# The first remainder's products ahead of two blocks of packs, and a remainder's output rows split by partitions between two engines

## The chip, the cores and the metric

The kernel runs on one core of one Trainium2 chip. The metric is the device time of one execution in microseconds (us), the median of several runs. A core has five engines that run side by side and wait for each other on semaphores: TensorE (PE in the profile, with its weight loads as PEld), VectorE (DVE), ScalarE (ACT), GpSimd (POOL) and SyncE (SP), which here only issues transfers. Transfers are carried out by 16 DMA engines that the issuing queues share.

## The reference

```python
def sm_attn(qq, kk, vv):
    s = scale * np.matmul(qq, kk.transpose(0, 1, 3, 2))
    s = s - np.max(s, axis=-1, keepdims=True)
    a = np.exp(s)
    a = a / (np.sum(a, axis=-1, keepdims=True) + 1e-09)
    return np.matmul(a, vv)
p_packed = sm_attn(p, k, v)
out = sm_attn(q, p_packed, p_packed)
...
x = out.transpose(0, 2, 1, 3).reshape(B * S, H * D)
h = x @ w_in
g = h * (1.0 / (1.0 + np.exp(-h)))
return g @ w_out
```

There are 8 batches of 8 heads, 576 tokens a batch, 64 elements a head, 32 packs a head; the model width is 512 and the inner width 2048. All arrays are fp32. Each head's 32 pack queries attend to all tokens, then all tokens attend to the 32 packed results; a two-layer network with a SiLU between follows on every token.

## The kernel before, in words

**Packs and h.** The second attention's values are multiplied with `w_in` before they are weighted: `Packs.products` (through `heads`, L232) makes "packs", the packed values of a batch times a quarter (512 columns, 4 blocks of 128) of `w_in`. A block of packs fills one `ps_two` tile, of which there are two (two PSUM banks each). `Packs.upper` (L490, ACT) rounds it to an upper part `pw_hi`, `Packs.lower` (L493, DVE) writes the difference `pw_lo`; both read the tile, which is free after that. `h_products` (L525) multiplies packs with the token shares `a_hi`, `a_lo` and gives one 128-row block of h for all tokens of a batch. Products of fp32 precision are made of three products of rounded parts: upper with upper, upper with lower, lower with upper.

**Units.** A unit is a pair (batch, block f of 128 inner columns). A batch's 576 tokens are taken as two halves of 288; of each half the first 256 tokens (MAIN) go through `h_values` (L543, L545, ACT: g and its upper part g_hi) and `h_lower` (L551, DVE: g_lo), and the 32 left over (REST) are put aside in `rest`. `out_products` (L561) multiplies g with `w_out`, summing over the 16 blocks in two `ps_acc` tiles. For each pair of batches the tokens left over, 2 x 2 x 32 = 128, make up a remainder: four units of four blocks each, whose g lies ready in `rest`. For them `h_values` only copies g to g_hi (L535, ACT), `h_lower` makes g_lo (L551, DVE), and `out_products` issues 4 x 3 products into one bank. There are four remainders, those of batches 0, 2, 4 and 6 with the batch after each.

**Order.** The order of PE, DVE, ACT and SP is that of the program text. The first 32 units (all of batches 0 and 1) follow the list ORDER, written by hand; its end is `o30 o31 g32 b1 l32 v3 e31.0 pp11 pu11 e31.1 pl11 k3`: the output products of the last units, g_hi and g_lo of unit 32 (the first unit of the first remainder), the output rows, the packs of batch 2, quarter 0, and a load. After that a loop takes the units from 32 on (`n_early`). Unit 32 stands first there: `packs_in(2, 1, 2)` makes quarters 1 and 2 of batch 2 (both products, then upper and lower of each), then come its output products. For unit 33 `hidden_up_to(35)` first issues g_hi and g_lo of units 33, 34 and 35, then its output products follow. With unit 34 the h products of batch 2 begin (unit 36).

**Output rows of a remainder.** After its fourth unit `out_rows` copies the 128 rows of 512 columns from the bank to a tile `o`: the left 256 columns by ACT (L595), the right 256 by DVE (L596). Rows 0 to 31 are batch b, first half; 32 to 63 batch b, second half; then the same for batch b + 1. Four transfers (L600) of 32 rows each, 64 KB, write them to `out`; all on SP, except in the last remainder, where two of them are issued by ACT. The last remainder is the last work of the kernel.

Of the kernel before, what the change touches and what calls it, by code (L numbers as in the profile page):

```python
# [20 lines left out]
B, H, S, D = 8, 8, 576, 64  # L21
NP = 32
NI = H // 2
HS = S // 2
NB = HS // 32
DM = H * D
# [7 lines left out]
MAIN = HS // P * P  # L34
REST = HS - MAIN
# [48 lines left out]
def packed_attention_ffn(ctx: ExitStack, tc: tile.TileContext, pkT, qT, v, w_in, w_out, out):  # L84
# [13 lines left out]
    nc = tc.nc  # L98
# [32 lines left out]
    def sum_banks():  # L131
        return ps_acc.tile([P, 2, 512], F32, name="ps_acc")
# [333 lines left out]
    class Packs:  # L466
# [5 lines left out]
        def products(self):  # L472
            self.ps = two_banks()
            heads(
                lambda par: self.ps[:, par, : self.nf * P].rearrange("p (f n) -> p f n", n=P),
                made["packs", self.b],
                lambda r, i: win[r, self.f : self.f + self.nf, i].bitcast(F32),
            )
# [19 lines left out]
    n_early = len(units)  # L498
# [9 lines left out]
    def half_or_all(hf):  # L508
        return slice(0, 2) if hf is None else slice(hf, hf + 1)

    def h_products(u, hf=None):
        b, f, *more = units[u]
        ps = made["h", u, hf] = two_banks()
        p_hi, p_lo = made["pw", b, f // FJ]
        cols = slice(f % FJ * P, f % FJ * P + P)
        for h in range(2)[half_or_all(hf)]:
            if u < WHOLE:
                terms = ((p_hi.bitcast(F32), made["whole", h]),)
            else:
                a_hi, a_lo = made["a2", b, h]  # L520
                terms = (p_hi, a_hi), (p_hi, a_lo), (p_lo, a_hi)
            todo = [(p, a, par) for par in range(2) for p, a in terms]
            for n, (p, a, par) in enumerate(todo):
                bank = ps[:, h if hf is None else 0, :HS]
                nc.tensor.matmul(bank, p[:, par, cols], a[:, par], start=(n == 0), stop=(n == len(todo) - 1))  # L525

    def h_values(u, hf=None):
        b, f, *more = units[u]
        if hf is None or hf == 0:
            pool = gp_b if u > n_early and (u - n_early) % 3 == 1 else gp  # L530
            g_hi = pool.tile([P, 512], F32R, name="g_hi")
            g_lo = pool.tile([P, 512], F32R, name="g_lo")
            if more:
                g = rest[:, f : f + FJ].rearrange("p f e h s -> p (f e h s)")
                nc.scalar.copy(g_hi, g)  # L535
                hidden[u] = g, g_hi, g_lo
                return
            hidden[u] = g_hi.bitcast(F32) if u < WHOLE else gp.tile([P, 512], F32, name="g", bufs=1), g_hi, g_lo
        g, g_hi = (x.rearrange("p (h s) -> p h s", h=2) for x in hidden[u][:2])
        ps, to = made.pop(("h", u, hf)), rest[:, f, b % 2]  # L540
        if hf is not None:
            ps, to, g, g_hi = ps[:, 0], to[:, hf], g[:, hf], g_hi[:, hf]
        nc.scalar.activation(g, ps[..., :MAIN], AF.Silu)  # L543
        if u >= WHOLE:
            nc.scalar.activation(g_hi, ps[..., :MAIN], AF.Silu)  # L545
        nc.scalar.activation(to, ps[..., MAIN:HS], AF.Silu)  # L546

    def h_lower(u, hf=None):
        c = slice(0, 512) if hf is None else slice(256 * hf, 256 * hf + 256)
        g, g_hi, g_lo = hidden[u][-3:]  # L550
        nc.vector.tensor_tensor(g_lo[:, c], g[:, c], g_hi[:, c].bitcast(F32), ALU.subtract)  # L551
# [11 lines left out]
    def is_last(u):  # L563
        return u + 1 == len(units) or units[u + 1][0] != units[u][0] or len(units[u + 1]) > len(units[u])

    def first_of(u):

        while u and not is_last(u - 1):
            u -= 1
        return u  # L570

    def out_products(u, hf=None):
        b, f, *more = units[u]
        start = first_of(u)
        first = u == start
        if more:
            if first:
                acc[start, 0] = sum_banks()
            for n in range(FJ):
                products(acc[start, 0][:, 0], u, f + n, n, f + n == 0, f + n == NF - 1)  # L580
            return
        for h in range(2)[half_or_all(hf)]:
            if first:
                acc[start, h] = sum_banks()
            for k in range(2):
                products(acc[start, h][:, k], u, f, 2 * h + k, first, is_last(u))

    def out_rows(u, h):

        b, f, *more = units[u]  # L590
        sums = acc[first_of(u), h]
        if more:
            o = osb.tile([P, 2, DM], F32, name="o")
            half = DM // 2
            nc.scalar.copy(o[:, 0, :half], sums[:, 0, :half])  # L595
            nc.vector.tensor_copy(o[:, 0, half:], sums[:, 0, half:])  # L596
            for n, (e, h) in enumerate((e, h) for e in range(2) for h in range(2)):
                at = (b + e) * S + h * HS + MAIN
                rows = slice((2 * e + h) * REST, (2 * e + h) * REST + REST)
                (nc.scalar if n % 2 and b == B - 2 else nc.sync).dma_start(out[at : at + REST], o[rows, 0])  # L600
            return
        if ("o", b, h) in outs:
            o = outs.pop(("o", b, h))
            nc.vector.tensor_tensor(o, sums, o, ALU.add)
        else:
            o = osb.tile([P, 2, DM], F32, name="o")
            (nc.vector.tensor_copy if h else nc.scalar.copy)(o, sums)
        if f == NF - 1:
            at = b * S + h * HS
            nc.sync.dma_start(out[at : at + MAIN].rearrange("(k p) e -> p k e", p=P), o)  # L610
        else:
            nc.sync.dma_start(parts[b, h], o)

    def load_parts(b):
# [24 lines left out]
        "l": h_lower,  # L639
        "o": out_products,  # L640
        "e": out_rows,
        "b": load_parts,
    }
# [18 lines left out]
    def hidden_up_to(u):  # L662
        nonlocal done
        while done < min(u, len(units) - 1):
            done += 1
            if len(units[done]) == 2:
                h_products(done)
            h_values(done)
            h_lower(done)

    def packs_in(b, *quarters):
        both = [Packs(b, FJ * j, FJ) for j in quarters]
        for part in both:
            part.products()
        for part in both:
            part.upper()
            part.lower()
# [39 lines left out]
    for u in range(n_early, len(units)):  # L717
        b, f, *more = units[u]
        if more:
            if u == n_early:  # L720
                packs_in(2, 1, 2)
            else:
                hidden_up_to(u + 2)
            out_products(u)
            if f + FJ == NF:
                out_rows(u, 0)
            continue
        step = STEPS_AT.get(f) if b + 1 < B else None
        all_banks = step in ("scores1", "scores2") or f == PACKS_OWN or f == PACKS_NEXT and b + 1 < B
        if not all_banks:  # L730
            hidden_up_to(u + 2)
        if f == PACKS_OWN:
            packs_in(b, *((3,) if b == 2 else (2, 3)))
        if f == PACKS_NEXT and b + 1 < B:
            packs_in(b + 1, 0, 1)
        if step:
            step_of(b + 1, step)
        out_products(u)
        if f == NF - 1:
            for h in range(2):  # L740
                out_rows(u, h)
        if step == "packed":
            attention[b + 1].turned()
            attention[b + 1].packs()
# [43 lines left out]
```

## Time and profile before

| | |
|---|---|
| median of 3 runs | 710.75 us (709.83 to 710.82) |
| the profiled execution, its own time | 710.59 us |
| its span | 708.8 us |
| mean granted clock of TensorE | 0.996 |
| PE busy | 696.7 us, 98% |
| DVE busy / ACT busy | 332.4 us (47%) / 328.5 us (46%) |
| transfers in all | 65.20 MB |

The span reaches from the first to the last instruction of the profiled execution; its own time is 1.8 us longer. In the lines of a view L561 is line 561 of the kernel; "x12" counts instructions merged into a line; a bracket gives how long the engine stood idle before it and who released it. SPq and ACTq are the queues that issue transfers. Times within the span are counted from its start.

### The profile page before, as it was taken

Reading aid. Unit: us, or ns where it says so; the run is one execution under the profiler, and the core shown is the slowest. Engines: PE = TensorE matmul, PEld = TensorE weight load, DVE = VectorE, ACT = ScalarE, POOL = GpSimd, SP = SyncE. Lnnn points to the kernel's source line nnn. Section 1 sums busy time; section 2 is a strip of 40 time slices with the busy share of each in tenths; the row PEclk is TensorE's granted clock in tenths of the full one; section 3 lists DMA queues with packets and bytes.
Section 4 is the critical chain, followed back from the end, with each engine's and each line's share of the span. In section 5 each row is a group of like instructions: output and inputs, shape, how many; then the busy total and the mean of one; then the engine's idle time right before and its main releaser. Section 6 shows DMA issues by size and latency. Waiting matters only on the chain.

```text
span 708.8 us, 12103 instructions
## 1 busy us (share of the span) xinstructions
PE 696.7 (98%) x5060; PEld 564.7 (80%) x5060; DVE 332.4 (47%) x491; ACT 328.5 (46%) x614; POOL 21.0 (3%) x16
## 2 busy tenths in 40 slices
PE   8999999999999999999999999999999999999997
PEld 6647779877868888888888888878878788888886
DVE  4989985944642346332552315433362333622112
ACT  4896858634534325362542625453353533533221
POOL 0202020100000000000000000000000000000000
PEclk9999999999999999999999999999999999999999
DMA  9755653315032140302212022121301210010002
GB/s 356 304 205 198 222 218 149 125 60 193 0 130 82 34 147 1 127 21 84 75 60 83 18 88 75 41 87 36 144 1 64 79 35 2 1 59 1 1 1 74
DMA packets 30869, 65.20 MB, mean 92 GB/s; under 512 B 19296, under 2 KB 19296, under 8 KB 26464
## 3 DMA queue, kind: packets, MB, share of 16 engines
q1 hardware_dynamic: 30720, 64.30, 25.1%
q8 instruction: 40, 0.66, 0.4%
q10 hardware_dynamic: 96, 0.13, 0.1%
q14 instruction: 13, 0.11, 0.0%
HBM read 48.76 MB, written 11.53 MB: 85 GB/s over the span
## 4 chain that ended last, share of the span: by engine, by line
PE 91%; DVE 5%; ACT 2%; issue 1%; DMA 1%; DVEq 0%; ACTq 0%
PE ps_acc L561 55%; PE ps_two L525 27%; PE ps_two L232 6%; PE ps_two L330 1%; DVE win L198 1%; DMA kvq_t<-in_pkT 1%; PE ps_acc L232 0%; ACT tm L278 0%; DVE win L204 0%; ACT w_raw L192 0%; ACT w_raw L193 0%; DVE w_raw L198 0%; ACT L543 0%; DVE win L197 0%; DVE win L205 0%
## 5 line engine op out<-in xcount | busy, mean ns | idle before, releaser
L561 PE MATMUL ps_acc<-wo_hi,g_hi 128*128 128x512 f32 x560 | 222.5, 397 | 0.0
L561 PE MATMUL ps_acc<-wo_lo,g_hi 128*128 128x512 f32 x560 | 219.0, 391 | 0.0
L561 PE MATMUL ps_acc<-wo_hi,g_lo 128*128 128x512 f32 x560 | 219.0, 391 | 0.1
L551 DVE TENSOR_TENSOR g_lo<-g,g_hi 128x512 fp32r<-128x512 f32 x124 | 89.2, 720 | 256.5 <-ACT g_hi L545 256.4
L543 ACT ACTIVATE g<-ps_two 128x512 f32<-128x512 f32 x124 | 74.4, 600 | 265.4 <-PE ps_two L525 236.4
L525 PE MATMUL ps_two<-a_lo,pw_hi 128*128 128x288 f32 x528 | 156.2, 305 | 0.2
L525 PE MATMUL ps_two<-a_hi,pw_hi 128*128 128x288 f32 x496 | 147.1, 297 | 1.0 <-ACT rest L546 1.0
L525 PE MATMUL ps_two<-a_hi,pw_lo 128*128 128x288 f32 x496 | 145.9, 294 | 0.0
L561 PEld LDWEIGHTS ps_acc<-wo_hi,g_hi 128*128 128x128 f32 x560 | 105.1, 188 | 38.7 <-issue 19.4
L561 PEld LDWEIGHTS ps_acc<-wo_hi,g_lo 128*128 128x128 f32 x560 | 105.1, 188 | 23.7 <-DVE g_lo L551 0.8
L561 PEld LDWEIGHTS ps_acc<-wo_lo,g_hi 128*128 128x128 f32 x560 | 105.2, 188 | 18.0
L525 PEld LDWEIGHTS ps_two<-a_lo,pw_hi 128*128 128x128 f32 x528 | 99.2, 188 | 6.8 <-ACT rest L546 0.9
L525 PEld LDWEIGHTS ps_two<-a_hi,pw_hi 128*128 128x128 f32 x496 | 93.3, 188 | 5.6 <-ACT rest L546 1.3
L525 PEld LDWEIGHTS ps_two<-a_hi,pw_lo 128*128 128x128 f32 x496 | 93.2, 188 | 0.0
L545 ACT ACTIVATE g_hi<-ps_two 128x512 fp32r<-128x512 f32 x124 | 73.6, 593 | 7.8 <-PE ps_acc L561 7.8
L493 DVE TENSOR_TENSOR pw_lo<-ps_two,pw_hi 128x1024 fp32r<-128x1024 f32 x31 | 36.8, 1219 | 9.5 <-ACT pw_hi L490 9.5
L490 ACT CAST pw_hi<-ps_two 128x1024 fp32r<-128x1024 f32 x31 | 30.2, 1019 | 16.0 <-PE ps_two L232 16.0
L232 PE MATMUL ps_two<-win,ppT 64*32 64x512 f32 (+1 forms) x560 | 32.7, 559 | 2.6 <-DVE pw_lo L493 1.6
L546 ACT ACTIVATE rest<-ps_two 128x64 f32<-128x64 f32 (+1 forms) x132 | 30.4, 230 | 0.0
L232 PEld LDWEIGHTS ps_two<-win,ppT 64*32 64x32 f32 x560 | 8.2, 105 | 17.8 <-issue 10.3
L543 ACT ACT_TABLE_LOAD x16 | 20.5, 1283 | 2.0 <-PE ps_two L525 1.9
L535 ACT CAST g_hi<-rest 128x512 fp32r<-128x512 f32 x16 | 9.9, 623 | 14.1 <-PE ps_acc L561 13.7
(116 smaller groups left out, 479.4 us busy)
## 6 DMA issues: line engine op xcount, KB each, us to landing
kvq_t<-in_v SPq DMA_DIRECT2D x8, 1280.0 KB, 6.4
kvq_t<-in_pkT SPq DMA_DIRECT2D x7, 1216.0 KB, 6.9
out<-o SPq DMA_DIRECT2D x16, 512.0 KB, 2.8
kvq_t<-in_qT SPq DMA_DIRECT2D x7, 1152.0 KB, 5.2
w_raw<-in_w_in SPq DMA_DIRECT2D x6, 1024.0 KB, 6.4
win<-in_w_out SPq DMA_DIRECT2D x3, 1024.0 KB, 5.7
w_raw<-in_w_out SPq DMA_DIRECT2D x3, 1024.0 KB, 4.8
tm<-tm SPq DMA_DIRECT2D x56, 40.0 KB, 1.9
```

Of the source, the lines that this page charges most:

```text
L198: nc.vector.scalar_tensor_tensor(low, up, -(2**31), low, op0=ALU.bitwise_and, op1=ALU.bitwise_or)
L232: nc.tensor.matmul(bank(par)[NP * i : NP * i + NP], lhs(r, i), rhs(r, i), start=True, stop=True)
L330: nc.tensor.matmul(self.ps[NP * i : NP * i + NP, par * D : par * D + D], e, vs[:n, c, h * D : h * D + D], start=(c == 0), stop=(c == 4),)
L490: nc.scalar.copy(self.hi, self.ps[:, :, : self.nf * P])
L493: nc.vector.tensor_tensor(self.lo, self.ps[:, :, : self.nf * P], self.hi.bitcast(F32), ALU.subtract)
L525: nc.tensor.matmul(bank, p[:, par, cols], a[:, par], start=(n == 0), stop=(n == len(todo) - 1))
L535: nc.scalar.copy(g_hi, g)
L543: nc.scalar.activation(g, ps[..., :MAIN], AF.Silu)
L545: nc.scalar.activation(g_hi, ps[..., :MAIN], AF.Silu)
L546: nc.scalar.activation(to, ps[..., MAIN:HS], AF.Silu)
L551: nc.vector.tensor_tensor(g_lo[:, c], g[:, c], g_hi[:, c].bitcast(F32), ALU.subtract)
L561: nc.tensor.matmul(bank, g[:, rows], w[:, at], start=(first and n == 0), stop=(last and n + 1 == len(todo)))
```

## The change

It has two parts. In the loop over units, unit 32's output products are issued before `packs_in(2, 1, 2)` and not after it. In `out_rows` a remainder's rows are split by partitions and not by columns: rows 0 to 63 (batch b) are copied whole by ACT, rows 64 to 127 (batch b + 1) by DVE, and each 64 rows leave with one transfer, whose destination is written as halves x 32 tokens x 512 columns. In the last remainder ACT issues the first of the two, elsewhere SP issues both.

```diff
@@ -591,13 +591,11 @@
         sums = acc[first_of(u), h]
         if more:
             o = osb.tile([P, 2, DM], F32, name="o")
-            half = DM // 2
-            nc.scalar.copy(o[:, 0, :half], sums[:, 0, :half])
-            nc.vector.tensor_copy(o[:, 0, half:], sums[:, 0, half:])
-            for n, (e, h) in enumerate((e, h) for e in range(2) for h in range(2)):
-                at = (b + e) * S + h * HS + MAIN
-                rows = slice((2 * e + h) * REST, (2 * e + h) * REST + REST)
-                (nc.scalar if n % 2 and b == B - 2 else nc.sync).dma_start(out[at : at + REST], o[rows, 0])
+            for e in range(2):
+                rows = slice(2 * e * REST, 2 * e * REST + 2 * REST)
+                (nc.vector.tensor_copy if e else nc.scalar.copy)(o[rows, 0], sums[rows, 0])
+                to = out[(b + e) * S : (b + e) * S + S].rearrange("(h s) e -> h s e", s=HS)[:, MAIN:]
+                (nc.sync if e or b < B - 2 else nc.scalar).dma_start(to, o[rows, 0])
             return
         if ("o", b, h) in outs:
             o = outs.pop(("o", b, h))
@@ -717,11 +715,11 @@
     for u in range(n_early, len(units)):
         b, f, *more = units[u]
         if more:
+            if u > n_early:
+                hidden_up_to(u + 2)
+            out_products(u)
             if u == n_early:
                 packs_in(2, 1, 2)
-            else:
-                hidden_up_to(u + 2)
-            out_products(u)
             if f + FJ == NF:
                 out_rows(u, 0)
             continue
```

## The prediction

> **What bounds the kernel now.** First the page's busy times, then the chain of waits, then the timeline where the two parts of the change lie: the change of stage near 194 us and the end.
>
> ```profile
> span 708.8 us, 12103 instructions
> PE 696.7 (98%) x5060; PEld 564.7 (80%) x5060; DVE 332.4 (47%) x491; ACT 328.5 (46%) x614; POOL 21.0 (3%) x16
> ```
>
> PE is busy nearly always. The chain of waits over 204.6 to 704.4 us, grouped by line, says how strictly:
>
> ```profile
> by line: PE ps_acc L561 61.4%; PE ps_two L525 30.6%; PE ps_two L232 6.2%; PE ps_two L330 1.7%; PE ps_two L349 0.1%
> ```
>
> For 500 us the chain is PE alone. A delay of PE before 204.6 us therefore comes out at the end in full, and so does a gain. What may move the time is a stall of PE ahead of that, or the work behind the last product. The chain at the change of stage:
>
> ```profile
> 195.41 1.02 ACT pw_hi L490
> 196.43 0.03 issue
> 196.46 1.23 DVE pw_lo L493
> ...
> 198.83 5.71 PE ps_acc L561 x24
> ```
>
> Here the chain leaves PE for ACT and DVE. The same stretch in the timeline, three engines together:
>
> ```profile
> 192.08 0.69 DVE L551 TENSOR_TENSOR g_lo<-rest,g_hi 128x512 fp32r<-128x512 f32 x1 [0.69 <-ACT g_hi L535]
> 194.21 1.95 PE L232 MATMUL ps_two<-win,ppT 64*32 64x512 f32 x32
> 195.41 1.93 ACT L490 CAST pw_hi<-ps_two 128x1024 fp32r<-128x1024 f32 x2 [3.36 <-PE ps_two L232]
> 196.46 2.36 DVE L493 TENSOR_TENSOR pw_lo<-ps_two,pw_hi 128x1024 fp32r<-128x1024 f32 x2 [0.91 <-ACT pw_hi L490]
> 197.73 1.09 PE L232 MATMUL ps_two<-win,ppT 64*32 64x512 f32 x16 [1.57 <-DVE pw_lo L493]
> 198.75 0.19 PEld L561 LDWEIGHTS ps_acc<-wo_hi,g_hi 128*128 128x128 f32 x1 [0.84 <-issue]
> 198.76 0.50 PE L561 MATMUL ps_acc<-wo_hi,g_hi 128*128 128x512 f32 x1
> 199.84 1.15 ACT L535 CAST g_hi<-rest 128x512 fp32r<-128x512 f32 x2
> 201.12 1.89 DVE L551 TENSOR_TENSOR g_lo<-rest,g_hi 128x512 fp32r<-128x512 f32 x3
> 201.61 0.39 PE L561 MATMUL ps_acc<-wo_hi,g_hi 128*128 128x512 f32 x1
> 204.38 0.29 PE L525 MATMUL ps_two<-a_hi,pw_hi 128*128 128x288 f32 x1
> ```
>
> The 32 products at 194.21 are two blocks of packs: the last of the written order (batch 2's quarter 0) and quarter 1. Quarter 2 needs the first one's bank back, which L490 and then L493 must read, so PE stands for 1.57 us. Then twelve products of remainder unit 32 run from 198.76 to 201.61 (2.85 us), and twelve of unit 33 follow without a gap. Those of unit 33 need its g_hi (L535) and g_lo (L551), which stand on ACT and DVE behind the packs' casts and differences. So unit 32's products cover unit 33's operands today.
>
> **First part: the order.** Unit 32's products go ahead of quarters 1 and 2 on PE. No transfer moves, and nothing is passed on SP or POOL. ACT and DVE keep their order: two packs, then unit 33.
>
> Unit 32 can run at once: its g_lo was done at 192.77. From 194.21 the first block takes 1.03 us up to the next product (198.76 minus 197.73), so unit 32 starts at 195.24 and ends at 198.09. By then L493 has freed the bank (196.46 + 1.23 = 197.69): the 1.57 us stall goes. What is late next is unit 33:
> - quarter 1 starts at 198.1; ACT gets it 1.20 later (195.41 minus 194.21), at 199.3;
> - ACT takes 1.93 for the two casts, to 201.2, then 0.6 for g_hi of unit 33, to 201.8;
> - DVE starts 1.05 after ACT (196.46 minus 195.41), at 200.35, needs 2.36 for the two differences and 0.63 (a third of 1.89) for g_lo, to 203.3;
> - PE finishes both quarters at about 200.1 (1.95 after 198.1), waits until 201.9 for g_hi, does the two products that need g_hi alone, and waits again for g_lo. The third starts at 203.5, after a weight load of 0.19. Ten are left: 10 x 2.85/12 = 2.4 at most, or 2.3 at the later spacing (201.61 to 204.38 for twelve).
>
> The next h products start at 203.5 + 2.3 = 205.8 instead of 204.38: **+1.4 us**. The wait is not removed; unit 33 has lost its cover. If the weight load is hidden it is 1.2, if handing over takes a little more 1.7.
>
> **Second part: the end.** Timeline, the longest waits, and the transfer share in slices:
>
> ```profile
> 704.57 0.37 ACT L595 COPY o<-ps_acc 128x256 f32<-128x256 f32 x1 [7.81 <-PE ps_acc L561]
> 704.98 0.42 DVE L596 COPY o<-ps_acc 128x256 f32<-128x256 f32 x1 [7.49 <-ACT o L595]
> 705.43 0.80 SPq L600 DMA_DIRECT2D out<-o  x2
> 705.43 0.87 ACTq L600 DMA_DIRECT2D out<-o  x2
> DVE o L596 <- ACT o L595: 11.5, 4, 7.5
> 706.10:706.20 0.10, 0.00 (x0) 0.00 (x0) 0.00 (x0) 0.00 (x0) 0.00 (x0) 1.00 0.00 0
> 706.20:706.30 0.10, 0.00 (x0) 0.00 (x0) 0.00 (x0) 0.00 (x0) 0.00 (x0) 1.00 0.49 123
> 706.30:707.30 1.00, 0.00 (x0) 0.00 (x0) 0.00 (x0) 0.00 (x0) 0.00 (x0) 0.63 0.92 246
> 707.30:707.40 0.10, 0.00 (x0) 0.00 (x0) 0.00 (x0) 0.00 (x0) 0.00 (x0) 0.50 0.16 41
> ```
>
> In a slice the last two numbers are the mean share of the 16 DMA engines and the GB/s. The column halves run one behind the other, all four times. The first transfer is issued at 705.43, data flow from 706.20 (0.77 later) to 707.4, and 1.4 us remain to the end of the span. Durations for copies of 512 columns, and for 64 rows against 128, from the groups by line:
>
> ```profile
> L315 DVE COPY tm<-ps_acc 128x512 f32<-128x512 f32 x1 | 0.7, 683 | 0.0
> L315 ACT COPY tm<-ps_acc 128x512 f32<-128x512 f32 x1 | 0.6, 571 | 0.0
> L316 DVE COPY tm<-ps_acc 64x128 f32<-64x128 f32 x1 | 0.3, 271 | 0.0
> L353 DVE COPY ppT<-ps_two 128x128 f32<-128x128 f32 x6 | 1.7, 290 | 13.6 <-PE ps_two L349 13.6
> ```
>
> Rows hardly count, columns do: 0.57 on ACT, 0.68 on DVE. ACT ends at 705.14, and its transfer needs its own copy alone: issue at about 705.17, data from 705.94. DVE ends at 705.25 beside ACT, or at 705.86 behind it; no row shows two engines reading one bank in different rows, so both stay open. The Trainium skill, "PSUM — Partial Sum Buffer", section on bank collisions, says that two engines may read one bank at once only in different groups of 32 partitions; by it the copies run side by side.
>
> What decides is the transfers' shape. A transfer of 32 rows today starts with a count of 32. The new destination is written with counts 2, 32, 512, and its rows of the two halves lie too far apart to be merged. Rows that bear on it, ACT's queue and the two stores of 512 KB:
>
> ```profile
> q10 hardware_dynamic: 96, 0.13, 0.1%
> 694.50:695.00 0.50, 0.50 (x4) 0.42 (x3) 0.50 (x2) 0.00 (x0) 0.00 (x0) 1.00 1.05 410
> ```
>
> ACT's two transfers have 64 rows of 2 KB and left 96 packets: 32 more, 16 for each transfer, which fits one closing packet from each of 16 engines. Every transfer here starts with a count that 16 divides, so none shows what a first count of 2 does. If the queue deals out whole steps of the first count, two engines carry everything, and both transfers may fall on the same two. A finer cut would need a second level of which no row shows a sign; I take the cut by the first count as five to six times as likely. The price: 4 x 64 KB = 262 KB. A busy engine moves 410/16/1.05 = 24.4 GB/s in the large stores, so two take 5.4 us; at the tail's own 246/16/0.92 = 16.7 GB/s they take 7.9. I take the first, since the new transfers queue 2 KB rows back to back as the large stores do. Data end at 705.94 + 5.4 = 711.3 instead of 707.4: **+3.9 us**, at most +6.4. DVE's copy doesn't matter then: the second transfer is issued long before the first has drained.
>
> The Trainium skill, "DMA: Bandwidth & Descriptors", section on why a DMA adds 16 to its semaphore, states that the engine count is the largest number up to 16 that divides the slowest dimension of both sides, and that they are the lowest-numbered ones; this speaks against the change, and the sum by it is the one above, by its absence the first rival. No run here shows it yet.
>
> The three earlier remainders lie beside PE work. Around the first:
>
> ```profile
> 214.82 0.60 ACT L543 ACTIVATE g<-ps_two 128x512 f32<-128x512 f32 x1 [1.22 <-PE ps_two L525]
> 218.75 0.37 SPq L158 DMA_DIRECT2D kvq_t<-in_qT  x1
> ```
>
> A copy longer by 0.2 fits into the 1.22 us that ACT waits anyway. A store that drains for 5.4 us instead delays the next load, q, by a microsecond or two, and q is used eight units later, over 30 us. Without that cover a load would come up to 5 us late. Nothing counted.
>
> **Sum.** The profiled execution took 710.6, 1.8 more than its span and 0.2 under the median of the three. 710.6 + 1.4 + 3.9 = **715.9 us**.
>
> **Rivals.**
> 1. *Not slower: sixteen engines all the same.* The queue cuts by rows, whatever the first count. Then the 1.2 us of data start 0.26 earlier, at 705.94: the end gains 0.1 (copies in turn) to 0.3 (side by side), and 710.6 + 1.4 - 0.3 = 711.7, no change that counts. It decides where the share of the engines passes 2/16. For it: packets are 2 KB rows in any case. Against: the first count is the only one whose cut the packets show. Chance 0.15.
> 2. *Each queue has its own two engines.* Then 131 KB take 2.7 us, to 708.7: +1.3, in all 713.3. Chance 0.06.
> 3. *The order costs nothing*, because unit 33's operands pass the packs or start sooner. 714.5. Against: both lists keep the packs ahead. Chance 0.05. That the order gains its 1.57 us outright besides would take this and rival 1 together.
> 4. *The clock falls in the new stall.* Rows of an early stretch with little PE work, granted clock third from last, and of the present stall:
>
> ```profile
> 27.00:28.00 1.00, 0.93 (x3) 0.68 (x4) 0.97 (x3) 0.98 (x2) 0.00 (x0) 0.65 1.06 451
> 28.00:29.00 1.00, 1.00 (x4) 0.60 (x3) 0.97 (x3) 0.54 (x1) 0.00 (x0) 0.50 1.04 440
> 193.00:205.00 12.00, 10.43 (x83) 6.65 (x82) 7.79 (x8) 4.60 (x6) 0.00 (x0) 1.00 0.52 193
> ```
>
> It fell to 0.50 for about 3 us there; 1.57 us of stall left it at 1.00, but the new stall is some 2.8 us in 3.5, with two products between. Half speed for 3 us costs 1.5: 717.4. Chance 0.2.
>
> **How the numbers follow.** The forecast keeps 0.54. Its own bounds are 1.2 to 1.7 and 3.5 to 6.4. The range 713.2 to 718.8 takes in rivals 2, 3 and 4 and leaves out rival 1 and the worst rate together with a fallen clock, some 0.18. A measurement here tells about 0.2% (1.4 us) from no change. Every case but rival 1 (0.85) is slower; of rival 1 about 0.10 lies within, 0.03 above and, with the order's gain, 0.02 below. So slower 0.88, same 0.10, faster 0.02.
>
> **What would show it.** Right: no wait of PE before quarter 2, but PE and its weight loads waiting near 200 us for L535 and then L551, and h products starting near 205.8; at the end two transfers, a DMA share near 0.13 for over 5 us. Wrong: a share above 0.13 there; unit 33 following the packs without a wait; or two waits elsewhere. If the clock column falls below 1.00 at 203 to 207, it is rival 4.

## The result, and the profile after

The changed kernel takes 719.7 us (median of 4 runs, 717.8 to 720.7) against 710.8 for the kernel before on the same chip: ratio 1.0126, 95% interval 1.011 to 1.0142. It is slower by some 9 us; the forecast was slower by 5, with 718.8 as the upper end.

The profiled execution has a span of 718.3 us, 9.5 more than before. Two places hold nearly all of it. The chain of waits and the timeline at the change of stage:

```profile
194.40 1.02 PE ps_two L232 x16
195.42 2.96 PE ps_acc L561 x12
198.38 1.10 PE ps_two L232 x16
199.48 0.02 issue
199.50 1.02 ACT pw_hi L490
200.53 0.02 issue
200.55 2.36 DVE pw_lo L493 x2
202.91 0.61 DVE g_lo L551
203.52 0.04 issue
203.56 4.14 PE ps_acc L561 x10
207.70 1.60 PE ps_two L525 x12
```

```profile
202.10 0.47 PE L561 MATMUL ps_acc<-wo_hi,g_hi 128*128 128x512 f32 x1 [1.84 <-ACT g_hi L535]
203.56 0.50 PE L561 MATMUL ps_acc<-wo_hi,g_lo 128*128 128x512 f32 x1 [0.76 <-DVE g_lo L551]
207.54 0.29 PE L525 MATMUL ps_two<-a_hi,pw_hi 128*128 128x288 f32 x1
```

The 1.57 us wait before quarter 2 is gone. In its place the chain leaves PE once for ACT, then runs through three differences of DVE (two of packs and unit 33's g_lo), and PE waits 1.84 us for unit 33's g_hi and 0.76 for its g_lo. The ten products after that take 4.14 us; twelve took 2.85 before. The slices of that stretch (granted clock third from last) say why:

```profile
203.00:204.00 1.00, 0.44 (x2) 0.40 (x3) 1.00 (x2) 0.00 (x0) 0.00 (x0) 1.00 0.00 0
204.00:205.00 1.00, 1.00 (x4) 0.78 (x3) 0.71 (x2) 0.00 (x0) 0.00 (x0) 0.51 0.00 0
205.00:206.00 1.00, 1.00 (x4) 0.73 (x3) 0.00 (x0) 0.00 (x0) 0.00 (x0) 0.50 0.00 0
206.00:207.00 1.00, 1.00 (x4) 0.81 (x3) 0.00 (x0) 0.00 (x0) 0.00 (x0) 0.50 0.00 0
207.00:208.00 1.00, 1.00 (x6) 0.87 (x6) 0.00 (x0) 0.00 (x0) 0.00 (x0) 0.79 0.00 0
```

For 3.4 us, from 204.0 to about 207.4, TensorE has half its clock: a product every 0.43 us in place of 0.23. From the first packs' product to unit 36's first h product it takes 13.21 us (194.33 to 207.54) instead of 10.17 (194.21 to 204.38): +3.04.

From there PE is alone on the chain again, as before; the way to the last product is 499.78 us instead of 499.72. The end, in the timeline, among the longest waits, in slices (share of the 16 DMA engines and GB/s last), and in ACT's queue:

```profile
707.32 0.39 PE L561 MATMUL ps_acc<-wo_hi,g_lo 128*128 128x512 f32 x1
707.79 0.58 ACT L596 COPY o<-ps_acc 64x512 f32<-64x512 f32 x1 [7.80 <-PE ps_acc L561]
708.40 1.14 ACTq L598 DMA_DIRECT2D out<-o  x1
708.40 0.69 DVE L596 COPY o<-ps_acc 64x512 f32<-64x512 f32 x1 [7.69 <-ACT o L596]
709.12 0.59 SPq L598 DMA_DIRECT2D out<-o  x1
```

```profile
709.60:709.80 0.20, 0.00 (x0) 0.00 (x0) 0.00 (x0) 0.00 (x0) 0.00 (x0) 1.00 0.08 20
709.80:716.80 7.00, 0.00 (x0) 0.00 (x0) 0.00 (x0) 0.00 (x0) 0.00 (x0) 0.70 0.12 36
716.80:717.00 0.20, 0.00 (x0) 0.00 (x0) 0.00 (x0) 0.00 (x0) 0.00 (x0) 0.50 0.08 31
```

The 7.0 us in the middle are not even. The same stretch in finer slices, its start, a late slice and its end:

```profile
710.00:711.00 1.00, 0.00 (x0) 0.00 (x0) 0.00 (x0) 0.00 (x0) 0.00 (x0) 1.00 0.13 14
715.00:716.00 1.00, 0.00 (x0) 0.00 (x0) 0.00 (x0) 0.00 (x0) 0.00 (x0) 0.50 0.13 49
716.00:717.00 1.00, 0.00 (x0) 0.00 (x0) 0.00 (x0) 0.00 (x0) 0.00 (x0) 0.50 0.08 33
```

```profile
q10 hardware_dynamic: 66, 0.13, 0.1%
```

A share of 0.12 is two engines of sixteen, and both transfers are in flight: one pair serves both queues. ACT's queue now carries 64 rows in 66 packets, so two closing packets where each transfer of 32 rows had sixteen. The data flow for 7.3 us instead of 1.2: slowly at first (14 GB/s), then at 35 to 49 GB/s, and in the last microsecond mostly on one engine (share 0.08). DVE still starts when ACT is done, although the two read different rows. From the last product's start to the end of the span it takes 10.98 us instead of 4.70 (704.10 to 708.8): +6.28. With 0.12 from ahead of the stretch this makes 0.12 + 3.04 + 0.06 + 6.28 = 9.5.

### The profile page after: what moved, and what is told of

Same layout as the page of the kernel before. It is cut to its first block, busy times and chain, and to the rows that moved or that the text cites. A ratio compares the mean times of both kernels' runs of the same rounds, so it can differ in the third digit from the quotient of the medians.

```text
span 718.3 us, 12095 instructions
## 1 busy us (share of the span) xinstructions
PE 697.9 (97%) x5060; PEld 564.7 (79%) x5060; DVE 333.5 (46%) x491; ACT 329.8 (46%) x614; POOL 21.0 (3%) x16
## 4 chain that ended last, share of the span: by engine, by line
PE 90%; DVE 4%; ACT 2%; DMA 2%; issue 0%; ACTq 0%; DVEq 0%
PE ps_acc L561 55%; PE ps_two L525 27%; PE ps_two L232 6%; PE ps_two L330 1%; DMA w_raw<-in_w_in 1%; DMA kvq_t<-in_pkT 1%; PE ps_acc L232 0%; ACT tm L278 0%; ACT w_raw L192 0%; DVE win L198 0%; ACT w_raw L193 0%; DVE w_raw L198 0%; ACT L543 0%; DVE win L204 0%; DVE win L205 0%
## 5 line engine op out<-in xcount | busy, mean ns | idle before, releaser
L551 DVE TENSOR_TENSOR g_lo<-g,g_hi 128x512 fp32r<-128x512 f32 x124 | 89.3, 720 | 256.6 <-ACT g_hi L545 256.5
L366 DVE STREAM_TRANSPOSE tm<-ps_two 128x288 f32<-128x288 f32 x28 | 11.3, 454 | 10.6 <-PE ps_two L232 10.6
```

Of the source, the lines that this page charges most:

```text
L366: nc.vector.transpose(t[:, par * HS : par * HS + HS], self.half[hf][:, par, :HS])
```

## The experiments

Each has its edit against the kernel before unless said otherwise; ratios are to the kernel before on the same chip (medians 709.8 to 710.7), with 95% intervals. The theory: the order moves the wait to unit 33 and so halves the clock, and the first count of 2 puts the output on two engines. The rivals stand with each.

**The order alone.** The second hunk of the diff, nothing else.

> The first part alone: unit 32's products ahead of quarters 1 and 2, the output rows as before. Theory (the stall moves to unit 33 and halves the granted clock for about 3 us): PE waits some 1.8 us for L535 and 0.8 us for L551 near 202 us, the clock column shows 0.50 from about 204 to 207, the h products of unit 36 start near 207.5 instead of 204.4, and the time is 713.7 (710.7 + 3.0). Rival (the first part costs only its stall, and the slow stretch in the changed kernel came from the transfers): the clock stays at 1.00 and the time is 712.2. Rival that the order is neutral by itself: 710.7.

712.9 us, ratio 1.0038 (1.0026 to 1.005), 2.7 us slower. Its timeline has the same waits of PE (1.8 us for L535, 0.8 for L551). In slices:

```profile
199.60:202.40 2.80, 0.70 (x2) 0.30 (x2) 2.63 (x3) 2.60 (x5) 0.00 (x0) 0.99 0.49 205
202.40:205.60 3.20, 2.82 (x7) 2.24 (x8) 1.53 (x3) 0.00 (x0) 0.00 (x0) 0.50 0.00 0
205.60:206.60 1.00, 1.00 (x6) 0.82 (x5) 0.00 (x0) 0.00 (x0) 0.00 (x0) 0.93 0.00 0
```

The clock is at 0.50 throughout the 3.2 us of the middle slice without the new transfers, so they are not its cause. From the first packs' product to the h products it takes 13.01 us (193.55 to 206.56), +2.84. The theory holds for this execution. The fall does not come every time: of the six executions the shortest (712.2 us) has a mean clock of 1.000, which leaves no room for it; the profiled one has 0.998.

**The rows alone.** The first hunk alone.

> The second part alone: rows split by partitions, two transfers per remainder with a first count of 2, the order as before. Theory (two engines carry both transfers): data flow for about 7 us at a DMA share of 0.12 to 0.14 after the last product, from the last product's start to the end of the span it takes 11.0 us instead of 4.7, and the time is 717.0 (710.7 + 6.3). Rival (the end was slow because the first part disturbed something, such as the clock): less than 713. Rival that the three earlier remainders delay PE as well: over 718.

717.1 us, ratio 1.0092 (1.0077 to 1.0107), 6.5 us slower; its data stretch:

```profile
706.40:712.40 6.00, 0.00 (x0) 0.00 (x0) 0.00 (x0) 0.00 (x0) 0.00 (x0) 0.50 0.12 38
```

The last product starts at 703.63, the span ends at 714.7: 11.07 us, 6.37 more than before and so nearly all of the loss. The three earlier remainders cost nothing that shows: the last product of before starts at 704.10. The two parts add up: 2.7 + 6.5 = 9.2.

**One transfer with a first count of 4.**

```diff
+            to = out[b * S : b * S + 2 * S].rearrange("(g s) e -> g s e", s=HS)[:, MAIN:]
+            nc.sync.dma_start(to, o[:, 0])
```

in place of the two transfers, the row copies as in the change.

> As the second part alone, but all 128 rows of a remainder leave with one transfer from SP, whose destination has a first count of 4 (four halves of 32 rows) in place of 2. Same bytes, same copies, one issue. Theory (the first count sets the number of engines): the DMA share is 0.25 in the end's data stretch, 262 KB at twice the rate take 3.5 us in place of 7, and the time is 713.5 to 714. Rival (a long list of rows in one transfer is slow whatever the count): 7 us or more, 717 or more. Rival (the number of transfers matters and not the engines): share near 1 and the time near 711.

714.5 us, ratio 1.0054 (1.0039 to 1.0069). The data stretch, and SP's queue on the page:

```profile
707.00:710.00 3.00, 0.00 (x0) 0.00 (x0) 0.00 (x0) 0.00 (x0) 0.00 (x0) 0.88 0.22 42
710.00:710.60 0.60, 0.00 (x0) 0.00 (x0) 0.00 (x0) 0.00 (x0) 0.00 (x0) 0.50 0.26 102
```

```profile
q1 hardware_dynamic: 30576, 64.43, 25.3%
```

The share rises to a quarter: four engines. The packets fit as well: before, 30720 + 96 in both queues, of which 16 transfers of 32 + 16 make 768 and leave 30048; here 4 transfers of 128 + 4 make 528, and 30048 + 528 = 30576. The size was missed at first: for 3 us these engines move 42 GB/s (25, 20 and 82 in the three), and only then 102, so that the end takes 8.49 us (704.21 to 712.7) where I had expected below 8.

**Row copies, four transfers.** The row copies of the change; for each 64 rows two transfers of 32 rows, on the same queue.

> The rows copied by 64 an engine as in the change, but four transfers of 32 rows, each with a first count of 32, two from each queue in the last remainder. Theory (the loss at the end is the engine count; the copies cost little): DVE still waits for ACT, its copy ends 0.5 later than before, data flow for about 1.2 us at a share near 0.9, and the time is 711.0 to 711.3. Rival (the row copies themselves or their order cost the 6 us): 716 to 717.

710.8 us, ratio 1.0008 (0.9998 to 1.0017): no change that can be told. The copies in the timeline, then the data stretch in slices:

```profile
704.66 0.58 ACT L596 COPY o<-ps_acc 64x512 f32<-64x512 f32 x1 [7.81 <-PE ps_acc L561]
705.27 0.69 DVE L596 COPY o<-ps_acc 64x512 f32<-64x512 f32 x1 [7.69 <-ACT o L596]
```

```profile
706.20:707.40 1.20, 0.00 (x0) 0.00 (x0) 0.00 (x0) 0.00 (x0) 0.00 (x0) 0.83 0.65 174
```

The share is below the 0.9 expected, and data flow until 707.6. DVE waits for ACT here too, and it hardly matters: from the last product's start to the end it takes 4.8 us (704.19 to 709.0). The 6 us belong to the engine count, not to the copies.

**Both narrow transfers from SP.** `nc.sync` for both in the rows alone.

> As the second part alone, but SP issues both of the last remainder's transfers, first count 2 each. Theory (one pair of engines serves both queues, and its rate for 2 KB rows is what it is): data flow at a share of 0.12 for about 7 us as with two queues, the start is later by at most 0.7 us, and the time is 716.5 to 717.5. Rival (two queues that alternate on the same engines slow each other down, and that is why a busy engine moved 20 GB/s where the large stores have 24): the data take about 5.4 us and the time is 715 to 715.5.

717.0 us, ratio 1.0095 (1.008 to 1.011). Data at 37 GB/s, as with two queues:

```profile
706.60:712.60 6.00, 0.00 (x0) 0.00 (x0) 0.00 (x0) 0.00 (x0) 0.00 (x0) 0.51 0.12 37
```

So the low mean rate does not come from two queues that alternate. The slow start is there too: 14 GB/s from 707 to 708.

**One narrow transfer.** As the rows alone, but DVE's 64 rows leave in two transfers of 32 rows.

> As the second part alone, but only the first 64 rows leave in one transfer with a first count of 2; the other 64 leave in two transfers of 32 rows from SP. Theory (both narrow transfers fall on one pair of engines, so they queue up): one alone drains in about 3.6 us, the end shortens by about 3 us against the second part alone, and the time is 713.5 to 714.2. Rival (each queue has its own pair): the first transfer needs the 7 us by itself, and the time stays near 717.

713.5 us, ratio 1.0049 (1.0032 to 1.0066). The end takes 7.86 us (703.54 to 711.4), 3.2 less than with two narrow transfers; from 708 the share is that of one pair, with what is left of the wide transfers on its two engines (SP's queue has packets until 710.1, ACT's until 709.9):

```profile
706.00:707.00 1.00, 0.00 (x0) 0.00 (x0) 0.00 (x0) 0.00 (x0) 0.00 (x0) 1.00 0.58 98
708.00:709.00 1.00, 0.00 (x0) 0.00 (x0) 0.00 (x0) 0.00 (x0) 0.00 (x0) 0.50 0.13 43
```

The narrow transfer takes 4.0 us of data (705.9 to 709.9), about half of the 7.3 for two, which a pair for each queue would not give. The rival of separate pairs falls.

**The order with a filler.** The order alone, and behind quarter 2:

```diff
+                for _ in range(7):
+                    nc.tensor.matmul(acc[u, 0][:, 1, :P], ident, ident, start=True, stop=True)
```

> The first part alone with seven products of the identity matrix behind quarter 2, written into a bank that nobody reads, so that PE works through most of its first wait of 1.8 us; the output rows as before. They add work that the reference doesn't need. Theory (the clock falls because PE stands for some 2.6 us within 3.5): the operands of unit 33 come as late as without the filler, but the granted clock stays at 1.00 and unit 33's last ten products take 2.3 us in place of 3.6; the time is 712.2, some 1.5 below the order alone. Rival (the clock falls for another reason, such as the load's traffic): it falls as before, and the time is 713.7 or more.

711.5 us, ratio 1.0018 (1.0009 to 1.0027). The operands come as late as before, but in slices:

```profile
202.00:203.00 1.00, 0.40 (x2) 0.36 (x3) 1.00 (x2) 0.03 (x1) 0.00 (x0) 1.00 0.00 0
204.00:205.00 1.00, 1.00 (x6) 0.81 (x5) 0.00 (x0) 0.00 (x0) 0.00 (x0) 1.00 0.00 0
```

The clock stays at 1.00. From the first packs' product to the h products it takes 11.63 us (193.37 to 205.00): +1.46 against before, the stall alone, and 1.4 less than the order alone. With PE at work in the first wait the clock does not fall: it fell because PE stood.

**The order with cover.** The order, and ahead of the packs:

```diff
             out_products(u)
             if u == n_early:
+                hidden_up_to(u + 1)
                 packs_in(2, 1, 2)
```

> The first part, and besides unit 33's g_hi and g_lo are issued ahead of quarters 1 and 2's casts and differences on ACT and DVE. The output rows as before. Theory (the first part failed because unit 33's operands stood behind the packs): PE has no wait from 194 us to the h products of unit 36, which start near 202.9 in place of 204.4; the clock stays at 1.00; the time is 709.2 (710.75 - 1.5). Rival (another wait comes, such as unit 34's operands or the bank of the packs): 710.7 to 711.5.

709.3 us, ratio 0.9978 (0.9969 to 0.9987), faster. The chain of waits:

```profile
193.48 1.02 PE ps_two L232 x16
194.50 2.96 PE ps_acc L561 x12
197.46 1.88 PE ps_two L232 x32
199.34 2.94 PE ps_acc L561 x12
202.28 1.60 PE ps_two L525 x12
```

PE does not leave the chain; from the packs to the h products 8.80 us (193.48 to 202.28) where the chain of before has 10.26 (194.28 to 204.54). The idea of the first part was sound; it lacked unit 33's operands.

**ACT alone copies.** One copy of 128 rows and 512 columns on ACT, four transfers as before.

> Before, but ACT alone copies a remainder's 128 rows of 512 columns in one instruction; four transfers as before. Theory (the two copies run in turn in both kernels because they read one bank, so splitting gains nothing): one copy takes 0.57 us in place of 0.37 + 0.42 in turn, the transfers are issued 0.25 us earlier, and the time is 710.5 (710.75 - 0.25), which can hardly be told from no change by time but can in the profile. Rival (the split helps): 711 or more.

709.6 us, ratio 0.9989 (0.998 to 0.9998).

```profile
704.66 0.59 ACT L594 COPY o<-ps_acc 128x512 f32<-128x512 f32 x1 [7.81 <-PE ps_acc L561]
705.27 0.80 SPq L598 DMA_DIRECT2D out<-o  x2
```

The transfers are issued 0.61 us after the copy's start instead of 0.86 (704.57 to 705.43). From the last product's start to the end it takes 4.4 us (704.19 to 708.6) instead of 4.70. Two copies in turn are worth less than one, but only by this 0.3 us; the ratio says 0.8, with an interval of 0.14 to 1.4 us that takes it in.

**Both.**

> The first part with unit 33's operands ahead of the packs, and ACT alone copying a remainder's rows. Theory: both gains add up, 710.75 - 1.5 - 0.25 = 709.0, faster than both kernels. Rival: one of them is taken back, 709.5 or more.

708.4 us, ratio 0.9973 (0.9962 to 0.9983): the fastest of all, faster than both kernels. By time it can't be told from the order with cover, whose interval overlaps; the profile shows both gains, with 4.36 us from the last product to the end (701.84 to 706.2).

## Why the prediction was wrong

**The order: right mechanism, right stall.** The wait went from quarter 2 to unit 33, first for L535, then for L551, and the filler measured it by itself: 1.46 us against 1.4 forecast.

**The clock: a rival that came true.** It was rival 4 with a chance of 0.2 and 1.5 us. The order alone lost 2.84 us, of which the filler gave 1.4 back. The step that failed is the weighing: the sum put the clock at nothing, because the stall of before, 1.57 us, had left it at 1.00, and I took that as evidence. But the new stall is 1.84 us and 0.76 more with two products between. The records of the clock show how the two differ. In every kept trace its changes stand whole multiples of 3.41 us apart, so time can be cut into steps of that length. These are the steps that hold the stalls in before, in the changed kernel, in the order alone and in the order with filler (PE's busy time stands behind the length):

```profile
194.55:197.96 3.41, 1.84 (x40) 0.49 (x32) 2.50 (x3) 1.93 (x2) 0.00 (x0) 1.00 0.79 297
200.60:204.01 3.41, 1.15 (x4) 0.70 (x5) 3.41 (x4) 2.39 (x4) 0.00 (x0) 1.00 0.47 200
198.92:202.33 3.41, 1.26 (x18) 0.30 (x2) 2.56 (x3) 3.29 (x5) 0.00 (x0) 1.00 0.57 232
199.00:202.41 3.41, 2.76 (x24) 1.94 (x16) 2.82 (x3) 3.03 (x5) 0.00 (x0) 1.00 0.68 282
```

PE was busy for 0.54, 0.34, 0.37 and 0.81 of the step, and in the step after it the clock fell in the second and the third case alone. At the ends of the twelve traces 0.40 (before) was still followed by a fall and 0.45 (the run with both gains) was not. Where a step begins differs from execution to execution, which may be why one execution of the order alone shows no fall; that was not tested. The Trainium skill, "TensorE: Matmul & The Clock Gate", part on the HAM clock gate, puts the fall behind an idle window of about 3.4 us; here PE was busy for about a third of the 3.41 us ahead of the fall, so the measurement asks for less.

The early stretch that I quoted, with a fall at 27.3 us, is no clear guide: in five of the twelve traces the clock fell there, in seven, the changed kernel and the order alone among them, it did not. The order alone over the whole of it:

```profile
20.00:35.00 15.00, 13.65 (x111) 9.15 (x113) 14.48 (x25) 12.87 (x27) 2.85 (x2) 1.00 0.75 298
```

In before PE was busy for 0.58 of the step ahead of that fall, more than the 0.54 that did not lower the clock at 195 us. So the busy share alone does not decide for every kind of work, and what else counts stays open.

**The end: right mechanism, the size missed.** Two engines carried everything and both queues shared them, as forecast; the Trainium skill's rule from "DMA: Bandwidth & Descriptors" agrees with the share of 0.12 for a first count of 2 and about 0.25 for 4, and with two and four closing packets. The term was 3.9 and measured 6.28. Its parts: the issue came 0.61 us after the copy's start, 0.60 forecast; data began about 1.3 us after the issue (709.7) instead of 0.77; they flowed for 7.3 us instead of 5.4; the rest was 1.3, near the 1.4 forecast. So the step that failed is the price of the data: I took 24.4 GB/s a busy engine from the large stores for the whole of it. That rate was reached only late (49/16/0.13 = 23.6 from 715 to 716). At the start the pair moved 14 GB/s for a microsecond, and from 716 to 717 one engine was mostly alone. The mean is 36/16/0.12 = 18.8, near the 16.7 of the small stores before, which I had quoted as the upper bound and not used.

**The range.** It left out the worst rate and a fallen clock together as unlikely. Both happened: 710.6 + 3.0 + 6.3 makes 719.9, and 719.7 was measured, 0.9 above the range. They are not rivals of each other, and added they belonged inside.

**Smaller points.** DVE waited for ACT in the new form as well. The Trainium skill's "PSUM — Partial Sum Buffer", section on bank collisions, would let them run side by side in different groups of 32 partitions; the trace shows a wait on a semaphore that the program sets, so it says nothing against the page. It cost little: with the copies alone changed, the end took 4.8 us instead of 4.70. Whether copies without that wait would help was not tried. The three earlier narrow stores delayed no PE work that shows: 499.78 us against 499.72 to the last product.

## What to carry to other kernels

When a step is moved ahead on one engine, look for what it had been covering: it is the next step's operands on the other engines that must move with it. Look at the first count of a store before reshaping it: here counts of 32, 4 and 2 were carried by sixteen, four and two engines, and a saved issue of 0.4 us is nothing against a store on two engines at the end of a kernel. When stalls of TensorE crowd into some 3.4 us so that it works for little more than a third of them, price them twice, once for themselves and once for half the clock behind them; the single stall of 1.57 us in the kernel before did not cost that.

## What the runs showed of the hardware beyond that

- A store with a first count of 2 took longer to issue: 1.14 us on ACT's queue and 0.59 on SP's, where two issues of 32 rows together took 0.87 and 0.80.
- Narrow stores start slowly: two engines moved 14 GB/s from 710 to 711 us and 35 to 49 later, four moved 25 and 20 in their first two microseconds and 102 later. Late in the transfer a busy engine moves what it moves in the large stores: 49/16/0.13 = 23.6 and 102/16/0.26 = 24.5, against 24.4. Why the start is slow was not settled; the alternation of two queues is ruled out, since both transfers from SP start alike.
- The closing packets of a transfer show in the queue's packet count: 66 for one transfer of 64 rows, 96 for two of 32 rows.
